# Attention passed SBUF to SBUF, w2's transpose moved, b2's gradient from ScalarE: one change to a transformer block's forward and backward pass

## The chip, the cores and the metric

The kernel runs on one core of a Trainium2 chip. A core has five engines that run side by side and meet at semaphores: TensorE (PE in the profile; PEld is its weight load), VectorE (DVE), ScalarE (ACT), GpSimd (POOL) and SyncE (SP). DMA transfers are issued from the queues of SP, POOL and ACT and are carried out by 16 DMA engines. The metric is the device time in microseconds of one execution; lower is better.

## The reference

One transformer block, forward and backward, in bfloat16, with S = 2048 positions, D = 512, F = 1792, and 32 heads of 16:

```python
h  = x + A(layernorm(x), wqkv, wo)
h2 = h + B(layernorm(h), w1, b1, w2, b2)

def A(x, wqkv, wo):            # W = 8 keys per query, 2 positions apart
    q, k, v = split(x @ wqkv)
    logits = einsum("bhsd,bhswd->bhsw", q, gathered k) * 16 ** -0.5
    logits = where(idx >= 0, logits, -1e9)      # idx = pos - 2 * (0..7)
    o = einsum("bhsw,bhswd->bhsd", softmax(logits), gathered v)
    return o @ wo

def B(x, w1, b1, w2, b2):
    return gelu(x @ w1 + b1) @ w2 + b2
```

The outputs are h2 and, for a given grad_out, the gradients of x, wqkv, wo, w1, b1, w2 and b2. The gradient of b2 is the sum of grad_out over the 2048 positions.

## The kernel before

The positions are worked on in four chunks of 512 (`CH`, `NC`). Most tiles have 128 partitions. The tile framework places waits and buffers, and orders each engine's instructions when the program is built; on the chip that order is fixed, so an instruction that waits holds up all behind it on its engine or queue. A tag with `bufs` buffers is a ring: a new tile waits until the readers of the old one are done.

Forward, per chunk c: `f_ln1` and `f_qkv` make q, k and v; `f_attn(c)` makes the softmax weights in two halves i (products `pa`, summed on PE into `lg`; `e`, exp on ACT, row sums `sm`, then `attn[c]`); `f_o(c)` multiplies the weights with v (`pbo`, eight products of 1.14 us pitch on DVE, L330), sums on PE (`pso`), copies to `otm` on ACT and transposes to `oT`; `f_h(c)` multiplies with wo, adds x, and makes the second layernorm and its transpose `ln2T`; `f_ffn1(c)` makes gelu in seven groups (ACT writes u, square and sigmoid; DVE z and g; POOL stores u, s and g to DRAM for the backward pass), and `f_ffn2(c)` multiplies with w2. The order in which they are written interleaves chunks: f_o(2), f_h(2), f_attn(3), then ffn1(2) mixed with ffn2(1), f_o(3), f_h(3), and so on.

The attention weights stand in `attn[c]` with 32 rows by four quarters in one layout, and the sums need them in `a4`, another spread over the partitions. Before, POOL stores them to DRAM (`at_r`, four DMAs, `put_q`, L442), and SP loads them back as `a4` (four DMAs, `att4`, L300); `a4` has one buffer. The backward pass reads at_r as well. `e` has two buffers of 2 KB a partition.

w2 is loaded twice: as it is (L587, on POOL, gated by exp of chunk 1) and transposed by a DMA on SP (L602, `w2T`, into the room of wqkv), held back by `gate(..., ("e", 3, 1))` until the second exp of chunk 3 has run. `turn_w_gen` transposes the four weights for the backward pass on PE, through one PSUM buffer (tag T), and stores them; it is taken in two steps of two.

Backward, first part (from about 282 us): `make_goutT` transposes grad_out on PE (through the same T buffer; ACT copies each pair of blocks, 128x1024, to SBUF, `to_T`, L276); `b1_gg` makes the gradient behind gelu, `b1_gx` that of the layernorm, and `gw2_gen`, taken step by step between, the gradient of w2. gw2_gen begins with b2's gradient: 16 matmuls of a column of ones with grad_out (L659), one copy on ACT and one store.

```python
    def f_o(c):
        a4 = att4(fr, at_r, CJ * c, CJ, f"a4_{c}", "a4", 1, 0)
```

Of the kernel before, what the change touches and what calls it, by code (L numbers as in the profile page):

```python
# [35 lines left out]
def kernel(  # L36
# [74 lines left out]
    def gate(ins, key):  # L111
        behind(ins, mark[key])
# [10 lines left out]
    nc.vector.memset(one_t[:], 1.0)  # L123
    ones_row = const.tile([1, P], BF16, name="ones_row")
    nc.vector.memset(ones_row[:], 1.0)
    ones_col = const.tile([P, 1], BF16, name="ones_col")
    nc.vector.memset(ones_col[:], 1.0)
    rstd1 = const.tile([P, NT], F32, name="rstd1")
    rstd2 = const.tile([P, NT], F32, name="rstd2")
    b1c = const.tile([P, FT], F32, name="b1c")  # L130
# [134 lines left out]
            nc.vector.tensor_scalar(out=dst[:, j, :], in0=src[:, j, :], scalar1=mv[:, j, 0:1],  # L265
                                    scalar2=r[:, j:j + 1], op0=ALU.subtract, op1=ALU.mult)

    def to_T(src, dst, nm, tag, tag2=None):
        for d2 in range(DC // 2):
            pt = ptile(f"pt{nm}{d2}", tag2 if tag2 and d2 else tag)  # L270
            for i in range(2):
                for j in range(TC):
                    dc = 2 * d2 + i
                    nc.tensor.transpose(pt[:, (i * TC + j) * P:(i * TC + j + 1) * P],
                                        src[:, j, dc * P:(dc + 1) * P], ident[:])
            nc.scalar.copy(out=dst[:, 2 * d2:2 * d2 + 2, :], in_=pt[:].rearrange("p (i t) -> p i t", i=2))  # L276


    def four(eng, pool_, d_t, t0, nj, name, tag, bufs, step, key=None):
# [63 lines left out]
    PRA, PRB = 4, 3  # L343
    oTs, hs, l2T = {}, {}, {}

    lT, k4s, q4s = {}, {}, {}

    def f_ln1(c):
        x = xs.pop(c)
# [67 lines left out]
    def f_attn(c):  # L417
        if c not in k4s:
            f_halo(c)
            f_k4(c)  # L420
            f_q4(c)
        k4, q4 = k4s.pop(c), q4s.pop(c)
        for i in range(TC // 2):
            lg = ltile(f"lg{c}_{i}")
            dots(fr, lg, q4, k4, i, f"{c}_{i}", HP[c], STEP[c])
            l4 = lg[:].rearrange("p j (w h) -> p j w h", w=W)
            mx = const.tile([P, 2, H], F32, name=f"mx{c}_{i}", tag="mx", bufs=2)
            nc.vector.tensor_reduce(out=mx[:], in_=lg[:].rearrange("p j (w h) -> p j h w", w=W), axis=AX.X, op=ALU.max)
# [11 lines left out]
            nc.vector.tensor_tensor(out=attn_v(c, i), in0=e[:],  # L440
                                    in1=sm[:].unsqueeze(2).to_broadcast([P, 2, W, H]), op=ALU.mult)
        put_q(pq, at_r, c, attn[c][:].rearrange("p s j m -> p s (j m)"))  # L442

    def f_o(c):
        a4 = att4(fr, at_r, CJ * c, CJ, f"a4_{c}", "a4", 1, 0)
        otm = fr.tile([P, TC, D], BF16, name=f"otm{c}", tag="qkv", bufs=2)
        for qd in range(Q4):
            v4 = row4(fr, v_r, qd, PAD + CJ * c - 2, CJ + 2, f"v4_{c}{qd}", "w4", 4, 0)
            ps = acc(f"pso{c}_{qd}")
            wsum(fr, ps, a4, v4, 0, f"o{c}_{qd}")  # L450
            mark["o", c, qd] = nc.scalar.copy(out=otm[:, :, qd * P:(qd + 1) * P], in_=ps[:].rearrange("p (j m) -> p j m", j=TC))
        pq.dma_start(out=tm(otm_d[c * CH:(c + 1) * CH, :]), in_=otm[:])
        oT = fr.tile([P, G, CH], BF16, name=f"oT{c}", tag="t2", bufs=2)
        to_T(otm, oT, f"o{c}", "U")
        oTs[c] = oT

    def f_h(c):
        x, oT = load_x(c, "xr"), oTs.pop(c)
        h = fb.tile([P, TC, D], BF16, name=f"h{c}", tag="h", bufs=2)
        for j in range(TC):  # L460
            ps = acc(f"psh{c}_{j}")
            for g in range(G):
                nc.tensor.matmul(ps[:], lhsT=oT[:, g, j * P:(j + 1) * P], rhs=wo[:, g, :], start=(g == 0), stop=(g == G - 1))
            nc.vector.tensor_tensor(out=h[:, j, :], in0=ps[:], in1=x[:, j, :], op=ALU.add)
        ln2 = fr.tile([P, TC, D], BF16, name=f"ln2_{c}", tag="t1", bufs=1)
# [125 lines left out]
    f_h(1)  # L591
    f_attn(2)
    turn_w = turn_w_gen()
    take(turn_w, 2)
    zero_pads(((q_r, S), (go_r, S), (at_r, S), (gl_r, S)), ("e", 1, 0))
    mix(f_ffn1(1), f_ffn2(0))
    f_o(2)
    f_h(2)
    take(turn_w, 2)
    f_attn(3)  # L600
    w2T = fw.tile([P, DC, F], BF16, name="w2T", tag="wq", bufs=1)
    gate(sync.dma_start_transpose(out=w2T[:], in_=B_w2[:, :]), ("e", 3, 1))  # L602
    mix(f_ffn1(2), f_ffn2(1))
    f_o(3)
    f_h(3)
# [10 lines left out]
    gb2 = br1.tile([1, D], BF16, name="gb2")  # L616
    for c in b1_order:
        gout[c] = br1.tile([P, TC, D], BF16, name=f"gout{c}")
    br2 = pool("br2", 1, side="right")

    def load_gout(c):
# [4 lines left out]
    def make_goutT(i):  # L626
        if i < NC:
            c = b1_order[i]
            goutT[c] = get(br1, [P, DC, CH], BF16, f"goutT{c}", "goutT", 2)
            to_T(gout[c], goutT[c], f"e{c}", "T")  # L630

    w1T_load = sync.dma_start_transpose(out=w1T[:], in_=B_w1[:, :])
    gate(w1T_load, ("r", 3))
# [20 lines left out]
        nc.vector.tensor_tensor(out=out_ap, in0=u[:], in1=resid, op=ALU.add)  # L654

    def gw2_gen():
        ps = acc("psb2", "A")
        for t in range(NT):
            nc.tensor.matmul(ps[0:1, :], lhsT=ones_col[:], rhs=gout[t // TC][:, t % TC, :], start=(t == 0), stop=(t == NT - 1))  # L659
        nc.scalar.copy(out=gb2[:], in_=ps[0:1, :])  # L660
        nc.scalar.dma_start(out=out_7.rearrange("(a d) -> a d", a=1), in_=gb2[:])
        for ft in range(FT):
            gtm = get(br1, [P, NT, P], BF16, f"gtm{ft}", "gtm", 2)
            sync.dma_start_transpose(out=gtm[:], in_=g_d[ft * P:(ft + 1) * P, :])
# [350 lines left out]
```

## Time and profile before

| what | us |
|---|---|
| five runs: 716.57, 715.1, 711.06, 714.37, 718.03; median | 715.1 |
| the profiled execution, its own time | 717.97 |
| its span, first to last instruction | 715.8 |
| PE busy (88% of the span) | 630.1 |
| DVE busy (78%) | 556.3 |
| ACT busy (55%) | 395.3 |
| POOL busy (29%) | 209.3 |

A row of a timeline reads: start, duration, engine, line, operation, output <- input, shapes, count, and in brackets how long the engine sat idle before and what ended that. A row of a tile's view reads: line, engine, operation, output <- input, count, then shortest, median and longest duration in ns, first and last start. PE's busy time counts overlapping matmuls once; one of 512 columns takes 379 ns from its start to its end, and a new one starts every 0.216 us. The granted clock is that of TensorE, 1.00 when full.

### The profile page before, as it was taken

How to read it: one execution, taken by the hardware profiler on the slowest of the kernel's cores; microseconds unless marked ns; L12 is line 12 of the kernel's file. 1: busy time of each engine (PE TensorE's matmuls, PEld its weight loads, DVE VectorE, ACT ScalarE, POOL GpSimd, SP SyncE). 2: the span in 40 equal slices, each digit the busy share in tenths (PEclk: the TensorE clock that was granted, in tenths of full speed). 3: DMA queues.
4: the chain of work that ended last, by engine and by line, in shares of the span. 5: the costliest groups of instructions: out<-in, count | busy, mean ns of one | idle time of the engine just before them, and what ended most of it. 6: DMA issues, size and time to landing. Idle time of an engine off the chain costs nothing.

```text
span 715.8 us, 10332 instructions
## 1 busy us (share of the span) xinstructions
PE 630.1 (88%) x3682; PEld 265.4 (37%) x3682; DVE 556.3 (78%) x919; ACT 395.3 (55%) x548; POOL 209.3 (29%) x318
## 2 busy tenths in 40 slices
PE   1898668779698499999999999999989999999985
PEld 0433222234243134444445444443523333334342
DVE  6467958778973849975988888386979999999655
ACT  4654325878957739945867676551222135357453
POOL 4324323534533432452443432313200310001000
PEclk9999897979989789999999999999999999999999
DMA  8497698664889769566775985849879998986632
GB/s 235 140 265 231 188 375 283 230 248 161 255 291 219 226 165 231 166 212 231 213 209 93 218 179 151 258 119 273 295 294 384 333 322 285 344 279 221 166 83 66
DMA packets 103221, 163.57 MB, mean 229 GB/s; under 512 B 60961, under 2 KB 69250, under 8 KB 103170
## 3 DMA queue, kind: packets, MB, share of 16 engines
q1 hardware_dynamic: 73824, 78.40, 39.2%
q0 software_dynamic: 24720, 80.07, 34.3%
q10 hardware_dynamic: 4626, 4.46, 1.9%
q8 instruction: 28, 0.46, 0.3%
q14 instruction: 23, 0.19, 0.1%
HBM read 90.97 MB, written 56.71 MB: 206 GB/s over the span
## 4 chain that ended last, share of the span: by engine, by line
PE 41%; DVE 18%; DMA 13%; issue 13%; ACT 9%; POOL 3%; SPq 2%; POOLq 0%; DVEq 0%; ACTq 0%
PE psy L892 5%; PE psw L788 5%; PE psq L370 4%; PE psq L929 4%; PE psw L667 3%; DVE pb L330 3%; PE psx L719 2%; DVE pa L313 2%; PE psf L506 2%; PE ps L535 2%; PE ga L320 2%; PE pss L336 2%; DMA v<-v_r 2%; DMA out_dram<-ow 2%; PE lg L320 1%
## 5 line engine op out<-in xcount | busy, mean ns | idle before, releaser
L330 DVE TENSOR_TENSOR pb<-ba,r 128x2048 bf16<-128x2048 bf16 x96 | 111.4, 1216 | 1.5 <-PE pss L336 1.0
L506 PE MATMUL psf<-ln2T,w 128*128 128x512 bf16 x224 | 58.9, 400 | 12.4 <-ACT u L508 12.3
L535 PE MATMUL ps<-w,g 128*128 128x512 bf16 x224 | 55.8, 379 | 0.0
L788 PE MATMUL psw<-h1tm,ln2a 128*128 128x512 bf16 (+1 forms) x256 | 54.3, 354 | 0.0
L667 PE MATMUL psw<-gout,gtm 128*128 128x512 bf16 x208 | 51.3, 379 | 1.8 <-DMA gtm<-g_d 1.0
L719 PE MATMUL psx<-w1T,gh 128*128 128x512 bf16 x216 | 50.4, 379 | 0.0
L330 DVE TENSOR_TENSOR pbo<-a,v 128x2048 bf16<-128x2048 bf16 x32 | 38.2, 1217 | 15.0 <-DMA a<-at_r 10.5
L372 ACT CAST qkv<-psq 128x512 bf16<-128x512 f32 x48 | 27.6, 586 | 32.7 <-PE psq L370 26.1
L697 PE MATMUL psg<-goutT,w2T 128*128 128x512 bf16 x168 | 42.3, 379 | 0.0
L508 ACT ACTIVATE u<-psf,b1c 128x512 bf16<-128x512 f32 x56 | 36.0, 681 | 8.5 <-PE psf L506 5.1
L313 DVE TENSOR_TENSOR pag<-go,bv 128x2048 bf16<-128x2048 bf16 x24 | 28.6, 1218 | 10.4 <-DMA go<-go_r 6.8
L506 PEld LDWEIGHTS <-w 128*128 128x128 bf16 x224 | 21.0, 101 | 42.1 <-issue 24.7
L710 POOL DMA_DIRECT2D h1tm_d<-th x27 | 20.6, 762 | 53.0 <-ACT th L708 37.2
L518 ACT ACTIVATE s<-z 128x1024 bf16<-128x1024 bf16 x28 | 29.6, 1060 | 11.7 <-DVE z L516 7.3
L863 ACT ACTIVATE gt<-pss 128x512 bf16<-128x512 f32 x32 | 19.1, 597 | 29.6 <-PE pss L336 29.6
L788 PEld LDWEIGHTS <-ln2a 128*128 128x128 bf16 x256 | 22.6, 98 | 29.8 <-issue 12.3
L708 ACT COPY th<-pth 128x1024 bf16<-128x1024 bf16 x27 | 27.0, 999 | 11.0 <-PE pth L706 11.0
L689 ACT ACTIVATE by<-bu 128x1024 bf16<-128x1024 bf16 x21 | 22.2, 1056 | 19.1 <-DVE gb1p L699 16.5
L892 PE MATMUL psy<-wqkvT,gT 128*128 128x512 bf16 x128 | 32.2, 383 | 0.1
L929 PE MATMUL psq<-gt,ln1a 128*128 128x512 bf16 x128 | 32.0, 380 | 0.0
L526 POOL DMA_DIRECT2D g_d<-g x28 | 20.6, 734 | 36.5 <-DVE g L520 34.5
L336 PE MATMUL pss<-pb,sel 128*32 128x512 bf16 x384 | 29.5, 384 | 1.5 <-DVE pb L330 1.2
(221 smaller groups left out, 1364.6 us busy)
## 6 DMA issues: line engine op xcount, KB each, us to landing
v<-v_r SPq DMA_DIRECT2D x16, 576.0 KB, 6.9
r<-go_r SPq DMA_DIRECT2D x16, 576.0 KB, 8.5
r<-k_r SPq DMA_DIRECT2D x16, 576.0 KB, 6.2
r<-q_r SPq DMA_DIRECT2D x16, 576.0 KB, 5.4
g_d<-g POOLq DMA_DIRECT2D x28, 256.0 KB, 4.0
h1tm_d<-th POOLq DMA_DIRECT2D x27, 256.0 KB, 4.4
h1tm<-h1tm_d POOLq DMA_DIRECT2D x3, 2048.0 KB, 13.6
x_d<-u POOLq DMA_DIRECT2D x21, 256.0 KB, 5.5
```

The costliest lines, as they stand in the source:

```text
L313: nc.vector.tensor_tensor(out=pr[:], in0=_ap(q_ap, [q_ap.ap[0], [P, 2], [0, W], [1, P]]), in1=_ap(k_ap, [k_ap.ap[0], [P, 2], [-DIL * P, W] ...
L330: last = nc.vector.tensor_tensor(out=pr[:], in0=_ap(a_ap, [a_ap.ap[0], [2 * H, CJ], [0, Q4], [1, H]], off=wh * H + (4 * H * wh if sg else 0)),
L336: mm = nc.tensor.matmul(ps[PR * n:PR * n + PR, :], lhsT=sel4[:], rhs=prs[wh][:, TC * n:TC * n + TC, :, :].rearrange("p j d h -> p (j d h)" ...
L506: nc.tensor.matmul(ps[:], lhsT=w1[0][:, dc, ft * P:(ft + 1) * P], rhs=ln2T[:, dc, :], start=(dc == 0), stop=(dc == DC - 1))
L508: nc.scalar.activation(out=u[:, i, :], in_=ps[:], func=ACT.Identity, bias=b1c[:, ft:ft + 1], scale=1.0)
L535: nc.tensor.matmul(ps[:], lhsT=gs[ft // 2][:, ft % 2, j * P:(j + 1) * P], rhs=w2[0][:, ft, :], start=(ft == 0), stop=False)
L667: nc.tensor.matmul(ps[:], lhsT=gtm[:, t, :], rhs=gout[t // TC][:, t % TC, :], start=(t == 0), stop=(t == NT - 1))
L697: nc.tensor.matmul(ps[:], lhsT=w2T[:, dc, ft * P:(ft + 1) * P], rhs=gT[:, dc, :], start=(dc == 0), stop=(dc == DC - 1))
L719: nc.tensor.matmul(ps[:], lhsT=t1s[ft // 2][:, ft % 2, j * P:(j + 1) * P], rhs=w1T[:, ft, :], start=(ft == 0), stop=(ft == FT - 1))
L788: nc.tensor.matmul(ps[:, 0:nf * P], lhsT=ln2a[:, t // TC, t % TC, dc * P:(dc + 1) * P], rhs=tmx[:, t, 0:nf * P], start=(t == 0), stop=(t = ...
L892: nc.tensor.matmul(ps[:], lhsT=gT[sel][:, g, j * P:(j + 1) * P], rhs=wqkvT[:, sel * G + g, :], start=(n == 0), stop=(n == NJ - 1))
L929: nc.tensor.matmul(ps[:], lhsT=ln1a[t // TC][:, t % TC, dc * P:(dc + 1) * P], rhs=gts[sel, t // TC][:, t % TC, :], start=(t == 0), stop=(t ...
```

## The change

Three parts. First, `f_attn` copies each half of the weights on DVE into a new tile `back`, with the four quarters in reverse order, and four DMAs on SP (`across`, which was there for q and k) carry `back` to `a4` from SBUF to SBUF. The stores to at_r stay, for the backward pass alone. `back` shares the two buffers of `e`; in the built program `back` has one of them and every `e` the other. Second, w2T is issued before `f_attn(3)`, gated by the h of chunk 1, and turn_w_gen is taken in steps of three and one. In the built program w2T stands on SP ahead of the transfers of a4 for chunk 2; POOL's load of w2 (L587), whose lines are not changed, comes ahead of the at_r stores of chunk 1. Third, ACT copies the transposed grad_out in halves that also give their row sums (`accum_out`), into `gb2p`; at the end of the stage the sums are added over the chunks, transposed on PE and stored. The matmuls with ones are gone.

```diff
-    def to_T(src, dst, nm, tag, tag2=None):
+    def to_T(src, dst, nm, tag, tag2=None, sums=None):
...
-            nc.scalar.copy(out=dst[:, 2 * d2:2 * d2 + 2, :], in_=pt[:].rearrange("p (i t) -> p i t", i=2))
+            if sums is None:
+                nc.scalar.copy(out=dst[:, 2 * d2:2 * d2 + 2, :], in_=pt[:].rearrange("p (i t) -> p i t", i=2))
+            else:
+                for i in range(2):
+                    nc.scalar.activation(out=dst[:, 2 * d2 + i, :], in_=pt[:, i * CH:(i + 1) * CH], func=ACT.Copy,
+                                         accum_out=sums[:, 2 * d2 + i, :])
...
             nc.vector.tensor_tensor(out=attn_v(c, i), in0=e[:],
                                     in1=sm[:].unsqueeze(2).to_broadcast([P, 2, W, H]), op=ALU.mult)
+            if i == 0:
+                back = fr.tile([P, Q4, TC, 2 * H], BF16, name=f"back{c}", tag="e", bufs=2)
+            o_ap, i_ap = back[:, 0, 2 * i, :], attn[c][:, 0, 2 * i, :]
+            st = 2 * H * TC
+            nc.vector.tensor_copy(out=_ap(o_ap, [o_ap.ap[0], [st, Q4], [1, 4 * H]]),
+                                  in_=_ap(i_ap, [i_ap.ap[0], [-st, Q4], [1, 4 * H]], off=(Q4 - 1) * st))
+        a4s[c] = fr.tile([P, CJ, 2 * H], BF16, name=f"a4_{c}", tag="a4", bufs=1)
+        across(a4s[c], back)
         put_q(pq, at_r, c, attn[c][:].rearrange("p s j m -> p s (j m)"))
 
     def f_o(c):
-        a4 = att4(fr, at_r, CJ * c, CJ, f"a4_{c}", "a4", 1, 0)
+        a4 = a4s.pop(c)
...
-            nc.vector.tensor_tensor(out=h[:, j, :], in0=ps[:], in1=x[:, j, :], op=ALU.add)
+            mark["h", c] = nc.vector.tensor_tensor(out=h[:, j, :], in0=ps[:], in1=x[:, j, :], op=ALU.add)
...
-    take(turn_w, 2)
+    take(turn_w, 3)
     zero_pads(((q_r, S), (go_r, S), (at_r, S), (gl_r, S)), ("e", 1, 0))
     mix(f_ffn1(1), f_ffn2(0))
     f_o(2)
     f_h(2)
-    take(turn_w, 2)
+    take(turn_w, 1)
+    w2T = fw.tile([P, DC, F], BF16, name="w2T", tag="wq", bufs=1)
+    gate(sync.dma_start_transpose(out=w2T[:], in_=B_w2[:, :]), ("h", 1))
     f_attn(3)
-    w2T = fw.tile([P, DC, F], BF16, name="w2T", tag="wq", bufs=1)
-    gate(sync.dma_start_transpose(out=w2T[:], in_=B_w2[:, :]), ("e", 3, 1))
...
-            to_T(gout[c], goutT[c], f"e{c}", "T")
+            to_T(gout[c], goutT[c], f"e{c}", "T", sums=gb2p[:, :, c:c + 1])
...
     def gw2_gen():
-        ps = acc("psb2", "A")
-        for t in range(NT):
-            nc.tensor.matmul(ps[0:1, :], lhsT=ones_col[:], rhs=gout[t // TC][:, t % TC, :], start=(t == 0), stop=(t == NT - 1))
-        nc.scalar.copy(out=gb2[:], in_=ps[0:1, :])
-        nc.scalar.dma_start(out=out_7.rearrange("(a d) -> a d", a=1), in_=gb2[:])
...
             br2.release()
             bt = pool("bt", 1)
+            nc.vector.tensor_reduce(out=gb2s[:], in_=gb2p[:], axis=AX.X, op=ALU.add)
+            nc.vector.tensor_copy(out=gb2b[:], in_=gb2s[:])
+            pth = ptile("ptg2", "T")
+            nc.tensor.transpose(pth[0:DC, 0:P], gb2b[:, :], ident[:])
+            nc.scalar.copy(out=gb2r[:], in_=pth[0:DC, 0:P])
+            pq.dma_start(out=out_7.rearrange("(dc p) -> dc p", p=P), in_=gb2r[:])
```

More of the change, by code (lines that the diff above doesn't have):

```diff
@@ L125 @@
     nc.vector.memset(ones_row[:], 1.0)
-    ones_col = const.tile([P, 1], BF16, name="ones_col")
-    nc.vector.memset(ones_col[:], 1.0)
     rstd1 = const.tile([P, NT], F32, name="rstd1")
@@ L344 @@
     oTs, hs, l2T = {}, {}, {}
-    lT, k4s, q4s = {}, {}, {}
+    lT, k4s, q4s, a4s = {}, {}, {}, {}
     def f_ln1(c):
@@ L615 @@
     place(br1, [P, D], BF16, "ow2", 3)
-    gb2 = br1.tile([1, D], BF16, name="gb2")
     for c in b1_order:
         gout[c] = br1.tile([P, TC, D], BF16, name=f"gout{c}")
+    gb2p = br1.tile([P, DC, NC], F32, name="gb2p")
+    gb2s = br1.tile([P, DC], F32, name="gb2s")
+    gb2b = br1.tile([P, DC], BF16, name="gb2b")
+    gb2r = br1.tile([DC, P], BF16, name="gb2r")
     br2 = pool("br2", 1, side="right")
```

## The prediction

> **What bounds the kernel now.** I read first the busy time by stretch (columns: length, busy us of PE, PEld, DVE, ACT, POOL, then granted clock, DMA share, GB/s), to see where TensorE (PE) is not full.
>
> ```profile
> 100.00:120.00 20.00, 12.16 (x61) 4.41 (x60) 12.80 (x20) 6.88 (x11) 4.32 (x7) 0.74 0.85 321
> 160.00:180.00 20.00, 19.98 (x107) 8.12 (x106) 17.48 (x30) 16.43 (x19) 8.21 (x12) 1.00 0.46 153
> 180.00:200.00 20.00, 13.42 (x109) 5.92 (x107) 19.05 (x27) 19.12 (x26) 11.51 (x16) 0.92 0.89 285
> 220.00:230.00 10.00, 10.00 (x46) 4.13 (x45) 2.41 (x4) 8.57 (x10) 3.63 (x5) 1.00 1.12 279
> 230.00:240.00 10.00, 3.68 (x11) 1.21 (x9) 7.87 (x11) 4.27 (x6) 3.13 (x5) 0.72 0.30 96
> 240.00:250.00 10.00, 5.22 (x46) 1.58 (x48) 8.88 (x12) 8.66 (x12) 5.55 (x8) 0.84 0.94 301
> 300.00:360.00 60.00, 59.25 (x346) 27.37 (x344) 46.14 (x106) 36.65 (x45) 25.68 (x37) 1.00 0.66 212
> 360.00:440.00 80.00, 78.11 (x454) 37.33 (x453) 68.65 (x160) 57.53 (x76) 31.34 (x45) 1.00 0.80 175
> ```
>
> From 300 on PE is full: work taken from PE there is time. In the forward it has holes, the largest at 230 to 250 (11.1 us idle). The timelines of SP, DVE and PE say what ends it:
>
> ```profile
> 94.92 4.49 SPq L300 DMA_DIRECT2D a<-at_r  x4
> 105.45 1.22 DVE L330 TENSOR_TENSOR pbo<-a,v 128x2048 bf16<-128x2048 bf16 x1 [4.03 <-DMA a<-at_r]
> ...
> 213.88 0.69 DVE L440 TENSOR_TENSOR attn<-e,sm 128x512 bf16<-128x512 f32 x1
> 210.94 9.82 SPq L602 DMA_TRANSPOSE w2T<-in_B_w_dram  x1
> 226.41 2.39 SPq L300 DMA_DIRECT2D a<-at_r  x4
> 231.33 1.22 DVE L330 TENSOR_TENSOR pbo<-a,v 128x2048 bf16<-128x2048 bf16 x1 [6.44 <-DMA a<-at_r]
> 236.95 3.57 PE L506 MATMUL psf<-ln2T,w 128*128 128x512 bf16 x8 [6.32 <-ACT u L508]
> ```
>
> Attention of chunk 3 is done at 214.5, its weighted sum (pbo) starts at 231.3: 16.8 us for SBUF to DRAM to SBUF, because w2T (issued 210.94, landing 16.7 later, at 227.6) fills the DMA engines (share 1.12). DVE's order is fixed, so z and g of ffn1(2) wait behind pbo, ACT's s behind them, PE behind u. Chunk 1 has the same in small (4.03). Chunks 0 and 2 show no such wait. The total:
>
> ```profile
> DVE pbo L330 <- DMA a<-at_r: 10.5, 2, 6.4
> ```
>
> **The change part by part**, in this profile's times; which instruction waits for which is read from the built program.
>
> *Chunk 1 (95 to 113).* The load of a_1 no longer waits for the at_r stores, but for the second copy into `back` (about 87) and for a4's only buffer, free when pbo of chunk 0 ends, 92.1. On SP it stands behind xr (86.87 to 88.8). Four issues at 0.6 (the row of k_first<-qkv, the same kind of transfer, 603 to 652 ns; landing 3.9 to 4.5) end at 94.5 and land by 99. DVE comes to pbo at 101.3: the 4.03 is gone. Late next is v_11, issued behind a_1 at 94.6 in place of 99.5; at the stretch's worst landing, 8.6, it is there at 103.2, just before its use. pbo stands ahead of chunk 0's layernorm, so all of ffn1(0) moves. On POOL the order also changes: the w2 load goes ahead of the at_r stores, as soon as the last reader of `early` is done (77.3 instead of 88.87). Two stores of at_r, four of q_r and two more of at_r queue behind it, but nobody in the forward waits for at_r now, and w2 no longer meets w1 (94.87). It meets the k_r stores at 82.5 instead, which xr waits behind; xr lands at 92.3 to 94 and is needed at 96.3, 2 us of cover. Bounds: 0 (w1 or v is late anyway) to 5.0 (4.03 and 1 more through v and q_r); nearer to the stall itself: **-3.5**.
>
> *Chunk 2 (156 to 214), w2T moved.* On SP w2T passes the loads of a_2, v_30..33, four output stores and xr. It waits for the last h of chunk 1 (157.1) and for 16 more PE transposes and two ACT copies (1.0 each) of the third weight, moved from 181 to 189 to where PE does ffn2(0). PE's order and the 1.7 us turn of the one T buffer put the last transpose at 162.8. So w2T issues 163 to 172.8 and lands at 179.7, while DMA share was 0.46: quieter, that holds. Against it: `e` has lost its second buffer to `back`, so e(2,1) waits for attn(2,0) and its copy. attn(2,1) moves from 167.5 to 171.4, its copy ends at 172.8, and a_2 issues 172.8 to 175.2 behind w2T. How long it then takes, bounds: 4.3 (a_3 in before, at the tail of w2T) to 9.9 (at_r stores beside w2T). Beside w2T it is nearer to the second: about 181.7. pbo(2) started at 179.4, so 2.3 late; behind it wait g_0, g_1 and with them u's ring. DVE still owes 1.0 more at that point (g_0, o, one reduction 2.15; pa 1.14 already done), and copies 0.35: 3.6 late at the end of pbo(2). Given back: ACT has two copies less (2.0) in a stretch where it is 19.1 of 20 busy, and PE's 13 score matmuls of chunk 3 (1.9) are no longer between the last pbo and psh. **+1.5**, between -1 (a_2 lands in 4.3) and +4 (nothing is given back).
>
> The Trainium skill speaks against this step too: "DMA: Bandwidth & Descriptors", section "Queues, rings and completion order", says that on each DMA engine descriptors are consumed in ring order, and SP has one ring there. By that rule a_2 can't overtake w2T: not before 179.7, and by the rule plus the 4.3 row 182 to 184, which would make this term about +2.
>
> *Chunk 3 (214 to 254).* attn(3,1) comes as before, right behind ln2(2), its copy (0.35) after it; a_3 issues over 2.4 and lands within 4.5: pbo at about 219 instead of 231.3 (both with chunk 2's delay left out). I then laid out DVE's and ACT's new order by row durations: pbo 1.14, z 0.34 and 0.60, g 0.60; u 1.2 a pair, square and sigmoid 0.96, table load 1.28, otm 0.5, oT 0.96. ACT then is the longer: 7 groups of 3.1, 4 otm, 2 oT, one load are 26.9 from u at 216.3, which with short waits ends oT at about 244 instead of 253.9. Late next: ACT itself. PE has 11.1 idle to give in 230 to 250. Bounds: -12 (DVE alone, 22 us of work from 219) to -4.5 (only the 6.44 stall, less two pbo of 1.14 that now stand ahead of z_0): **-9.5**, as ACT's rows are complete.
>
> *b2's gradient (282 to 345).*
>
> ```profile
> L659 PE MATMUL psb<-gout,ones_col x16: 377/378/379, 338.1 to 345.4; 128*1 128x512 bf16 x16
> 367.50 3.45 PE psw L667 x16
> L276 ACT COPY goutT<-pte x6: 988/1003/1012, 297.3 to 380.3; 128x1024 bf16<-128x1024 bf16 x6
> L646 ACT ACTIVATE luf<-psx x16: 576/597/604, 325.5 to 467.8; 128x512 f32<-128x512 f32 x16
> L646 ACT ACTIVATION_READ_ACCUMULATOR luf<-psx x16: 191/194/211, 326.0 to 468.3; 128x1 f32 x16
> ```
>
> Matmuls overlap; 16 of 512 columns cost 3.45 on the full PE (second line, from the chain): -3.45. Eight copies of 1.0 become 16 of 0.6 with 16 reads of 0.19: 4.6 us more on ACT, hidden where it is 61 to 72% busy (300 to 440), not in 289 to 300. There ACT's new order puts the second half of the first tile behind s, square and 1-s (3 x 0.96), and PE's transposes of the next tile wait for the one T buffer: pth(0) comes about 2 later. The other chunks: 0.4. The two small DVE ops, one transpose, copy and store at the end are beside gw2 (gb1's same ops took 0.2 each): 0. Bounds: -3.45 (all hidden) to +2. **-1.0**.
>
> *Copies into `back`*, 8 in all: no row of this shape; between 0.2 (the 14x128 copy, L834) and 0.62 (the strided 128x512 copy, L231). Taken 0.35, the pitch of a plain 128x512 bf16 op (L265, 4 in 1.38). Chunk 0's lie under DVE's 3.0 wait at 70.5; those of 2 and 3 are counted; chunk 1's: **+0.5**.
>
> Sum: -3.5 + 1.5 - 9.5 - 1.0 + 0.5 = -12.0. The profiled run took 717.97 (span 715.8), 2.9 over the median of 715.1: 706.0 for that run, **703** for the median.
>
> **Rivals.** (a) *Only stalls go*: ffn1's own chain holds chunk 3 and w1 holds chunk 1; -4.5 + 1.5 - 1 + 0.5 = -3.5, or -6 with 2.5 kept in chunk 1: 709 to 712. For: ACT 8.57 of 10 busy in 220 to 230. Against: it idles from 229.7 to 235.3. (b) *The ACT reads cost more than the matmuls*, +4 to +5 at 289 to 300: about 708. For: ACT is full there. Against: it is one turn of one buffer. (c) *Slower*: a_2 sits behind w2T so long that f_o(2) loses what f_o(3) gains. Its price is the landing of a_2 beyond 181.7, one for one, as DVE and ACT are full until 199; at the sum's -12 it decides from a landing 12 later, about 193.7, 19 us after issue, and shows as slower from 197. For: all DVE waits there. Against: the longest landing near, a q_r store, is 14.3. Price at 200: +6, 721. (d) *w2T doesn't move*, as it still waits for late transposes: excluded by the program's order, which has them before ln2(1). (e) *All shifts in full*, -12 and -5: 696.
>
> **How the numbers follow.** 0.5% (3.6 us) is what this kernel's runs can tell. Chances: forecast 0.56, a 0.19, b 0.12, c 0.06, e 0.07. Faster by over 0.5% (under 711.5): nearly all of the forecast, b and e, and half of a: 0.84; same 0.10; slower 0.06. Range: up to most of a (711), down to past e (695); c lies outside.
>
> **What would show it.** Right: no DVE wait for a at pbo of chunks 1 and 3; w2T issued near 160 (earlier by chunk 1's gain), PE busy over 7 of 10 in the stretch after ln2(2); PE's 16 psb gone, pth(0) late by 2. Wrong: a DVE wait of over 8 before pbo(2), or oT of chunk 3 following ln2T(2) by over 35 us (39.3 now, from 214.6 to 253.9), or psf waiting for w1 in chunk 0.

## The result, and the profile after

The changed kernel is slower, not faster: 720.8 us against 714.4 (medians of 28 and 47 executions), ratio 1.0078, 95% interval 1.0060 to 1.0095, that is 4.3 to 6.8 us more. All ratios here leave out slow executions, those over 1.5% above the fastest of their kernel (four of 28 of the changed kernel and none of the kernel before; four of twelve in run 15), so this one is below 720.8 over 714.4, which is 1.0090. Forecast were 703 and a gain of 12.

The traced execution of the changed kernel took 727.86, 7 over its own median, so of its numbers I use those that other traces repeat; run 4 below has the same forward code and a trace of 714.92, and stands beside it.

The first fence is SP's, ACT's, POOL's and DVE's timeline of the changed kernel, around chunks 1, 2 and 3 (start, duration, engine, line, operation, count, idle time before and what ended it; L598 is w2's load, L387 the transfer of back to a4):

```profile
80.28 1.12 POOL L598 DMA_DIRECT2D w<-in_B_w_dram  x1 [2.30 <-DMA v<-v_r]
81.95 2.18 SPq L177 DMA_DIRECT2D k_r<-qkv  x4
92.42 0.58 ACT L462 CAST otm<-pso 128x512 bf16<-128x512 f32 x1 [4.91 <-DMA k_r<-qkv]
97.79 3.21 SPq L387 DMA_DIRECT2D a<-back  x4
108.00 1.19 DVE L333 TENSOR_TENSOR pbo<-a,v 128x2048 bf16<-128x2048 bf16 x1
165.57 9.80 SPq L612 DMA_TRANSPOSE w2T<-in_B_w_dram  x1
176.16 4.45 SPq L387 DMA_DIRECT2D a<-back  x4
189.87 1.23 DVE L333 TENSOR_TENSOR pbo<-a,v 128x2048 bf16<-128x2048 bf16 x1 [9.62 <-DMA a<-back]
226.22 0.68 DVE L443 TENSOR_TENSOR attn<-e,sm 128x512 bf16<-128x512 f32 x1
232.68 2.36 DVE L333 TENSOR_TENSOR pbo<-a,v 128x2048 bf16<-128x2048 bf16 x2 [3.95 <-DMA a<-back]
```

Chunk 3 went nearly as forecast: pbo starts 6.5 after the start of the second half of attention, not 17.5, but a wait of 3.95 for a is left, where I had written down none. Chunk 1 has no wait for a any more, and yet its pbo starts at 108.00, where it was 105.45: now otm of chunk 0, the step before, is 6 us later, for it waits 4.91 for the k_r stores (3.91 in run 4). And chunk 2 has a new wait of 9.62 for a, which stands behind w2T (4.39 in run 4).

PE's holes lie elsewhere now. Busy time by stretch, first of the changed kernel and then of the kernel before (columns: length, busy PE, PEld, DVE, ACT, POOL, then granted clock, DMA share, GB/s):

```profile
180.00:200.00 20.00, 11.96 (x65) 4.47 (x64) 10.38 (x15) 11.22 (x13) 4.73 (x7) 0.82 0.77 197
200.00:220.00 20.00, 15.65 (x82) 6.71 (x83) 15.59 (x26) 17.36 (x23) 10.13 (x15) 0.76 0.93 329
230.00:240.00 10.00, 10.00 (x47) 4.25 (x45) 7.28 (x10) 9.63 (x12) 3.20 (x5) 1.00 0.38 118
240.00:250.00 10.00, 9.10 (x52) 3.40 (x50) 7.39 (x13) 9.68 (x14) 6.77 (x10) 1.00 0.93 294
```

```profile
200.00:220.00 20.00, 19.91 (x110) 8.62 (x103) 13.47 (x27) 10.69 (x13) 6.55 (x10) 0.91 0.90 258
```

230 to 250, where PE idled 11.1, is full (19.1 of 20). 200 to 220, which was full, has 4.4 idle, and 180 to 200, which had 6.6 idle before, has 8.0; DVE and ACT, which were full there, have 9 to 10 idle each. In run 4 the idle time of PE in the three is 4.6, 5.5 and 4.5.

Read from the ends of the transposes (ACT's rows), the pass divides into stretches. Each line is one traced execution; the ratio is over many.

| kernel | to ln2T(1) | ln2T(1) to ln2T(2) | ln2T(2) to oT(3) | the last two | ln2T(3) ends at | to first pth | ratio to the kernel before |
|---|---|---|---|---|---|---|---|
| before | 167.2 | 48.3 | 38.3 | 86.6 | 266.2 | 34.1 | 1 |
| changed | 171.9 | 57.7 | 29.7 | 87.3 | 271.8 | 37.0 | 1.0078 |
| run 4: changed, b2 by matmuls | 171.7 | 52.8 | 29.7 | 82.4 | 266.7 | 34.9 | 1.0022 |
| run 10: only attention | 170.0 | 51.0 | 30.2 | 81.2 | 263.2 | 34.2 | 1.0032 |
| run 11: only w2T | 167.9 | 56.2 | 29.7 | 85.9 | 265.8 | 34.4 | 1.0005 |
| run 9: only b2 | 166.9 | 47.9 | 37.9 | 85.8 | 265.0 | 37.0 | 1.0045 |
| run 3: changed, w2 later | 166.5 | 51.5 | 29.7 | 81.2 | 259.6 | 37.0 | 0.9972 |
| run 5: runs 2, 3 and 4 together | 167.8 | 48.5 | 34.7 | 83.2 | 263.5 | 34.2 | 0.9972 |
| run 6: runs 3 and 4 together | 166.9 | 51.2 | 29.7 | 80.8 | 260.3 | 35.0 | 0.9932 |
| run 15: only attention, w2 later | 163.1 | 47.5 | 36.8 | 84.3 | 259.7 | 34.1 | 1.0003 |
| run 7: before, w2 later | 166.5 | 52.6 | 31.8 | 84.4 | 263.2 | 34.2 | 0.9924 |
| run 8: before, one e | 169.9 | 51.2 | 30.1 | 81.3 | 263.1 | 34.4 | 0.9947 |

One trace is one draw: executions of one kernel differ by 1.5 to 4 us (standard deviation), and the changed kernel and run 4, with the same forward code, end ln2T(3) 5.1 apart. Verdicts below go by the ratios; the traces say where.

### The profile page after: what moved, and what is told of

Read it like the earlier page. It is cut to its first block, busy times and chain, and to the rows that moved or that the text cites. A ratio compares the mean times of both kernels' runs of the same rounds, so it can differ in the third digit from the quotient of the medians.

```text
span 726.1 us, 10328 instructions
## 1 busy us (share of the span) xinstructions
PE 634.6 (87%) x3667; PEld 266.5 (37%) x3667; DVE 556.6 (77%) x928; ACT 396.9 (55%) x572; POOL 210.0 (29%) x319
## 5 line engine op out<-in xcount | busy, mean ns | idle before, releaser
L517 PE MATMUL psf<-ln2T,w 128*128 128x512 bf16 x224 | 61.3, 412 | 10.1 <-ACT u L519 10.0
L676 PE MATMUL psw<-gout,gtm 128*128 128x512 bf16 x208 | 52.8, 388 | 7.3 <-DMA gtm<-g_d 5.5
L333 DVE TENSOR_TENSOR pbo<-a,v 128x2048 bf16<-128x2048 bf16 x32 | 38.2, 1214 | 22.7 <-DMA a<-back 13.6
L706 PE MATMUL psg<-goutT,w2T 128*128 128x512 bf16 x168 | 44.5, 393 | 0.0
L878 ACT ACTIVATE gt<-pss 128x512 bf16<-128x512 f32 x32 | 19.1, 596 | 27.3 <-PE pss L339 25.4
L708 DVE CUSTOM_DVE_ANT_0 gh<-psg,by 128x512 bf16<-128x512 f32 x42 | 27.9, 686 | 7.5 <-PE psg L706 7.0
L797 PEld LDWEIGHTS <-ln2a 128*128 128x128 bf16 x256 | 22.6, 98 | 28.4 <-issue 11.1
L676 PEld LDWEIGHTS <-gtm 128*128 128x128 bf16 x208 | 19.6, 99 | 34.7 <-issue 7.6
```

Source lines behind the costliest of these rows:

```text
L333: last = nc.vector.tensor_tensor(out=pr[:], in0=_ap(a_ap, [a_ap.ap[0], [2 * H, CJ], [0, Q4], [1, H]], off=wh * H + (4 * H * wh if sg else 0)),
L517: nc.tensor.matmul(ps[:], lhsT=w1[0][:, dc, ft * P:(ft + 1) * P], rhs=ln2T[:, dc, :], start=(dc == 0), stop=(dc == DC - 1))
L676: nc.tensor.matmul(ps[:], lhsT=gtm[:, t, :], rhs=gout[t // TC][:, t % TC, :], start=(t == 0), stop=(t == NT - 1))
L706: nc.tensor.matmul(ps[:], lhsT=w2T[:, dc, ft * P:(ft + 1) * P], rhs=gT[:, dc, :], start=(dc == 0), stop=(dc == DC - 1))
L797: nc.tensor.matmul(ps[:, 0:nf * P], lhsT=ln2a[:, t // TC, t % TC, dc * P:(dc + 1) * P], rhs=tmx[:, t, 0:nf * P], start=(t == 0), stop=(t = ...
```

## The experiments

**The three parts, one at a time.** Each of these kernels is the one before with one part of the change.

Run 9, b2's gradient alone:

```diff
-            to_T(gout[c], goutT[c], f"e{c}", "T")
+            to_T(gout[c], goutT[c], f"e{c}", "T", sums=gb2p[:, :, c:c + 1])
...
-        for t in range(NT):
-            nc.tensor.matmul(ps[0:1, :], lhsT=ones_col[:], rhs=gout[t // TC][:, t % TC, :], start=(t == 0), stop=(t == NT - 1))
...
+            nc.vector.tensor_reduce(out=gb2s[:], in_=gb2p[:], axis=AX.X, op=ALU.add)
...
```

> The kernel before with only b2's gradient taken from ScalarE's sums. Theory G (the 16 matmuls stood in a wait for the transposed g, gtm, and so cost nothing; the sums cost real time): PE waits 3 to 4 for gtm between 340 and 370, the first pth comes 36 to 38 after the last ln2T instead of 34.1, and the time is 3 to 5 over the kernel before: 718 to 720. Rival (my forecast): -1.0, 713 to 715. Rival order: the 4 between the two kernels with attention changed came from the order that the scheduler found there, and here it is 715 within 2.

Measured: 720.1 against 715.7, ratio 1.0045 (1.0004 to 1.0085), +3.2. The first pth comes 37.0 after the last ln2T, against 34.1. PE waits for gtm, the transposed g that the gradient of w2 needs, but 2.0 and not 3 to 4.

Run 10, attention alone:

```diff
+        a4s[c] = fr.tile([P, CJ, 2 * H], BF16, name=f"a4_{c}", tag="a4", bufs=1)
+        across(a4s[c], back)
...
-        a4 = att4(fr, at_r, CJ * c, CJ, f"a4_{c}", "a4", 1, 0)
+        a4 = a4s.pop(c)
```

> The kernel before with only attention's way changed; w2T's load and b2's gradient as before. What the other runs leave for it: the changed kernel less b2's part was 1.0022 of the kernel before, and putting w2T back changed nothing (1.0079 against 1.0078): 714 to 718. In the trace the wait of otm of chunk 0 for the k_r stores (4 to 5) with w2 issued near 80, and from ln2T(2) to oT(3) 30 instead of 38.3. Rival: w2T's new place cost 3 or more and the place of this kernel's own w2T none: 708 to 712.

Measured: 716.4 against 715.7, ratio 1.0032 (0.9996 to 1.0067), +2.3. Chunk 3's stretch is 8.1 shorter (30.2), chunk 2's 2.6 longer, and otm of chunk 0 waits 3.34 for the k_r stores; w2 is issued at 80.19.

Run 11, w2T's move alone:

```diff
-    take(turn_w, 2)
+    take(turn_w, 3)
...
-    take(turn_w, 2)
+    take(turn_w, 1)
+    w2T = fw.tile([P, DC, F], BF16, name="w2T", tag="wq", bufs=1)
+    gate(sync.dma_start_transpose(out=w2T[:], in_=B_w2[:, :]), ("h", 1))
     f_attn(3)
-    w2T = fw.tile([P, DC, F], BF16, name="w2T", tag="wq", bufs=1)
-    gate(sync.dma_start_transpose(out=w2T[:], in_=B_w2[:, :]), ("e", 3, 1))
```

> The kernel before with only w2T's load moved; a goes through DRAM and follows w2T on SP's queue in chunk 2. Theory: in chunk 3 the round trip no longer meets w2T, so pbo comes 8 to 11 after the second attn instead of 17.5, and that is worth up to 6.4; in chunk 2 a comes 2 to 5 later. Net -4 to 0: 711 to 715. Rival c of the prediction in its pure form (a behind w2T on one queue is late by 10): 718 or more, with a wait of over 8 ahead of pbo of chunk 2.

Measured: 715.5 against 715.7, ratio 1.0005 (0.9969 to 1.0041). Its timeline of SP and DVE in chunk 2:

```profile
163.13 13.54 SPq L601 DMA_TRANSPOSE w2T<-in_B_w_dram  x1
180.14 2.41 SPq L300 DMA_DIRECT2D a<-at_r  x4
187.66 1.23 DVE L330 TENSOR_TENSOR pbo<-a,v 128x2048 bf16<-128x2048 bf16 x1 [7.04 <-DMA a<-at_r]
```

w2T now keeps SP's queue busy from 163.1 to 176.7, a is issued behind it, and pbo starts 20.1 after the second half of attention (11.9 before). Chunk 2 takes 7.8 more and chunk 3 8.6 less: the stall has changed places, at no gain and no loss.

The three ratios add up to 1.0082; the change as a whole has 1.0078. So these runs show no fourth cost that only the three together make: +2.3, +0.4 and +3.2 of about 5.6. But each has an uncertainty of 2.5 to 2.9, so the sum has one of 4 to 5, and a cost or gain of that size could hide in it.

**The changed kernel with one thing undone.**

Run 1: w2T back at its old place in the code, with its old gate (run 11's diff the other way round).

> The changed kernel with w2T's load (and the fourth weight's transposes) put back where they were, behind attention of chunk 3 with its old gate; on SP's queue w2T then stands right ahead of chunk 3's a, not of chunk 2's. Theory Q (a stands behind w2T on SP's queue, and that alone makes it late): pbo of chunk 2 waits less than 2 us for a instead of 9.6 and starts near 181 to 184 (189.9 in the changed kernel); in chunk 3 the wait is back, pbo at 10 to 17 after the second attn, as in the kernel before (17.5). Sum against the kernel before: chunk 1 +2.3, chunk 2 0 to +2, chunk 3 -2 to 0: 714 to 719 us. Rival E (e's one buffer and the copies make attention of chunk 2 late, whatever w2T does): pbo of chunk 2 stays later than 187, oT of chunk 2 stays over 8 late, and with chunk 3's gain lost the time is 725 or more.

Measured: 721.1, ratio 1.0079 (1.0047 to 1.0110): the same as with w2T moved. The wait before pbo of chunk 2 is 0.45, as the first theory said, but chunk 3 stays short (30.0) although a now stands behind w2T there, and the time does not fall. Theory Q, that a's place behind w2T alone makes the loss, falls. Rival E falls too: pbo of chunk 2 is at 179.9, not after 187.

Run 2: w2T behind chunk 3's a.

```diff
-    take(turn_w, 1)
-    w2T = fw.tile([P, DC, F], BF16, name="w2T", tag="wq", bufs=1)
-    gate(sync.dma_start_transpose(out=w2T[:], in_=B_w2[:, :]), ("h", 1))
+    take(turn_w, 2)
     f_attn(3)
+    w2T = fw.tile([P, DC, F], BF16, name="w2T", tag="wq", bufs=1)
+    gate(sync.dma_start_transpose(out=w2T[:], in_=B_w2[:, :]), ("back", 3))
```

Here `mark["back", c]` is the copy into back, and turn_w is taken 2 and 2.

> As the one before, but w2T's load is gated behind the last copy into back of chunk 3, so that on SP's queue it follows a_3 and stands ahead of nothing that attention waits for. Theory Q: no wait of over 2 us for a in chunks 2 and 3; pbo of chunk 3 starts 5 to 7 us after its second attn instead of 17.5; chunk 3 gains 8 to 9, chunk 1 still costs 2.3, chunk 2 0 to 2: 706 to 711 us, about 0.8% under the kernel before. Rival C (contention: w2T's transfer fills all the DMA engines, and whatever is in flight beside it is late, in front of it in the queue or behind): pbo of chunk 3 waits over 4 us for a or v, or psg of the backward waits for w2T, and the time is 714 or more.

Measured: 718.4 against 715.1, ratio 1.0035 (1.0009 to 1.0061). Nothing that attention needs stands behind w2T now, and that is worth 0.43% of the changed kernel (0.3 to either side), not the 706 to 711 of theory Q.

Run 3: the gate of w2's load.

```diff
-    gate(pq.dma_start(out=w2[0][:], in_=B_w2.rearrange("(ft p) d -> p ft d", p=P)), ("e", 1, 0))
+    gate(pq.dma_start(out=w2[0][:], in_=B_w2.rearrange("(ft p) d -> p ft d", p=P)), ("o", 0, 0))
```

> The changed kernel with one key altered: the load of w2 waits for the first otm of chunk 0 instead of the first e of chunk 1, and so no longer stands ahead of attn's stores on POOL's queue. Theory: in the changed kernel w2's 1.8 MB (issued 80.3) meet the k_r stores (82.0), which land in 7.5 instead of 4.1 (medians); otm of chunk 0 waits 4.9 for them, as it takes over their buffer. Without that, otm(0) starts at 87 instead of 92.4, pbo of chunk 1 at 101 to 104 instead of 108.0, and the time falls by 3 to 6 from the changed kernel's 720.8: 715 to 718. Rival: the two big loads w1 and w2 meet again, psf of chunk 0 or ps of its second half waits for its weight, and the time stays at 720 or more.

Measured: 714.9, ratio 0.9972 (0.9941 to 1.0003), 1.06% or 7.6 us less than with the old gate. otm of chunk 0 is at 88.75 and no longer waits for the stores, which land in 2.6 (median of chunk 1's four, as far as the profile tells their landings; 8.9 in the changed kernel, 2.2 before, and not the 7.5 and 4.1 that I had written). pbo of chunk 1 starts at 105.2 (108.0 in the changed kernel; I had expected 101 to 104), and oT of chunk 1 is 4.2 earlier.

Run 4: b2 by matmuls again, the rest of the change kept (run 9's diff the other way round).

> The changed kernel with b2's gradient taken by the 16 matmuls again and the copies of goutT whole again. My step: the new way is worth 1.0, so this one is 1 slower: 721 to 723. Rival b of the prediction: ScalarE's 16 halves and 16 reads cost more than the matmuls (first pth 3.0 later, counted from the last ln2T: 35.1 before, 38.1 in the changed kernel), and this one is 1 to 3 faster: 718 to 720, with the first pth 35 after the last ln2T.

Measured: 716.8, ratio 1.0022 (0.9993 to 1.0052), 0.56% or 4.0 less than the changed kernel. The first pth is back at 34.9 after ln2T(3). Rival b of the prediction, at about its price there, and more than the 1 to 3 expected here.

**Together, and on the kernel before.**

Run 5: the changed kernel with runs 2, 3 and 4 together. Run 6: with runs 3 and 4, w2T where the change puts it. Their common part:

```diff
-    gate(pq.dma_start(out=w2[0][:], in_=B_w2.rearrange("(ft p) d -> p ft d", p=P)), ("e", 1, 0))
+    gate(pq.dma_start(out=w2[0][:], in_=B_w2.rearrange("(ft p) d -> p ft d", p=P)), ("o", 0, 0))
...
-            to_T(gout[c], goutT[c], f"e{c}", "T", sums=gb2p[:, :, c:c + 1])
+            to_T(gout[c], goutT[c], f"e{c}", "T")
```

> Attention SBUF to SBUF kept, and the three losses taken out: w2's load waits for the first otm of chunk 0, w2T's load follows a_3 on SP's queue, b2's gradient goes by the 16 matmuls again. If the three add up as measured singly (7.6, 2.4 to 3 and 4.0 under the changed kernel's 720.8): 705 to 708, 1.0 to 1.3% under the kernel before. Rival: the gate's gain and w2T's place are the same microseconds seen twice (both give chunk 2 a quieter stretch), and it is 709 to 712.

> The same, but w2T's load stays where the change put it, ahead of chunk 2's a. If a's place behind w2T costs about 2 in chunk 2 (ln2T of chunk 1 to ln2T of chunk 2: 50.4 and 50.8 with w2T elsewhere, 51.5 and 52.8 with it there, in the four runs so far), this one is 1 to 3 over its neighbour: 708 to 711. If place on the queue is free, the two are the same; if a lands 10 late as in the changed kernel's profiled run (9.6 of wait), it is 714 or more.

Measured: 712.8, ratio 0.9972 (0.9938 to 1.0005), and 710.4, ratio 0.9932 (0.9907 to 0.9958). Run 3 and run 4 together promise 0.992 for run 6, and that holds. But run 5, with a free of w2T, should have been the faster one and is not: the two differ by 0.40%, with 0.42 to either side. By this pair, a's place on the queue is worth nothing that these runs can tell; run 15 below is another.

Run 7: the kernel before with w2's gate altered alone, run 3's diff.

> The kernel before, with only w2's gate altered (first otm of chunk 0 instead of first e of chunk 1). Theory: the gate only undoes a harm of the change (w2's load pulled from 88.9 to 80.3, into the k_r stores), so on the kernel before, where w2 is issued after those stores anyway, it gives nothing: 713 to 717. Rival: a later w2, behind w1, is a gain by itself, whatever attention does: 707 to 711, and then most of the 7.6 that the gate gave on the changed kernel says nothing of the change.

Measured: 710.7 against 715.3, ratio 0.9924 (0.9892 to 0.9955). My theory was that the gate only undoes a harm of the change; the rival holds. A later w2 is a gain of 5.4 by itself, and most of run 3's 7.6 says nothing of the change. Its timeline of POOL and DVE:

```profile
96.20 0.78 POOL L584 DMA_DIRECT2D w<-in_B_w_dram  x1 [0.28 <-issue]
97.71 1.10 POOL L587 DMA_DIRECT2D w<-in_B_w_dram  x1
103.78 1.23 DVE L330 TENSOR_TENSOR pbo<-a,v 128x2048 bf16<-128x2048 bf16 x1 [2.15 <-DMA a<-at_r]
```

w1 (L584) goes ahead of w2 (L587), and a of chunk 1 comes 1.7 earlier than before, through DRAM. With attention SBUF to SBUF and the same gate pbo of chunk 1 starts at 105.2, 106.9, 106.1 and 103.6 (runs 3, 5, 6 and 15): not earlier than that, but for run 15.

Run 8: one buffer for e in the kernel before.

```diff
-    place(fr, [P, 2, W, H], F32, "e", 2)
+    place(fr, [P, 2, W, H], F32, "e", 1)
...
-            e = get(fr, [P, 2, W, H], F32, f"e{c}_{i}", "e", 2)
+            e = get(fr, [P, 2, W, H], F32, f"e{c}_{i}", "e", 1)
```

> The kernel before with one buffer for e instead of two, as the change leaves it (the other holds back). Theory: the two halves of attention of chunk 2 then come 7 to 9 apart (5.7 before; 7.2 to 8.9 in the changed kernel and its variants), and chunk 2 from ln2T(1) to ln2T(2) takes 49 to 51 instead of 48.3; nothing else: 716 to 718. Rival: with the round trip through DRAM still there, the second half's delay goes straight into a: 720 or more. Or there is slack, and it is 715 like the kernel before; then the 2 that chunk 2 loses with w2T at its old place come from the copies and across itself.

Measured: 711.9 against 715.3, ratio 0.9947 (0.9918 to 0.9977): faster, where the theories had it slower or the same. The halves of attention of chunk 2 come 8.7 apart (5.7 before) and chunk 2 takes 51.2, as foreseen; but chunk 3 takes 30.1 in place of 38.3, with the trip through DRAM in place.

Run 12: the diffs of runs 7 and 8 together.

> The kernel before with w2's gate altered and one buffer for e, each of which was faster by itself (0.9924 and 0.9947). If they take away different waits (the gate: w2 ahead of w1 and beside chunk 1's a; the one buffer: chunk 3's part, 30.1 instead of 38.3 from ln2T(2) to oT(3)), they add: 705 to 708. If both only shake the order that the scheduler found, so that the wait of 6.4 in chunk 3 falls elsewhere, it is gained once: 710 to 712.

Measured: 710.1 against 715.7, ratio 0.9916 (0.9878 to 0.9953). They do not add up; what the two gain is largely one and the same. It is the lowest ratio of all, but its interval overlaps those of runs 6 and 7.

**What was still open.** Run 13 takes the matmuls of b2 away and puts only a copy of one row of grad_out in their place, so that its gradient of b2 is not one:

```diff
-        ps = acc("psb2", "A")
-        for t in range(NT):
-            nc.tensor.matmul(ps[0:1, :], lhsT=ones_col[:], rhs=gout[t // TC][:, t % TC, :], start=(t == 0), stop=(t == NT - 1))
-        nc.scalar.copy(out=gb2[:], in_=ps[0:1, :])
+        nc.scalar.copy(out=gb2[:], in_=gout[3][0:1, 0, :])
```

Run 14 is run 9 with those lines kept, up to the copy to `gb2`, which is not stored:

```diff
     def gw2_gen():
+        ps = acc("psb2", "A")
+        for t in range(NT):
+            nc.tensor.matmul(ps[0:1, :], lhsT=ones_col[:], rhs=gout[t // TC][:, t % TC, :], start=(t == 0), stop=(t == NT - 1))
+        nc.scalar.copy(out=gb2[:], in_=ps[0:1, :])
```

> The kernel before without the 16 matmuls of b2's gradient and with nothing in their place (out_7 gets a row of grad_out): what taking them away is worth by itself. Theory G (they stand in a wait for gtm): 0 to -1.5 against the kernel before, 714 to 716, and the trace shows PE waiting 2 or more for gtm between 340 and 365, where the kernel before waits less. My step: -3.45, 711 to 712.

> The kernel before with the sums of the change and with the 16 matmuls kept as well (their result goes nowhere): what the sums cost by themselves. Theory G: about as much as the change of b2's part alone (1.0045), +2 to +4, 717 to 719, the first pth 36 to 38 after the last ln2T. My step: +0.4 to +2, 715.5 to 717. Rival: the cost lies in the order without the matmuls (psw and its gtm earlier), and with them in place it is 715 within 1.

Measured: run 13 713.4 against 714.3, ratio 0.9984 (0.9954 to 1.0014), -1.1; run 14 717.7, ratio 1.0056 (1.0031 to 1.0081), +4.0. So the sums cost 4.0 by themselves. Run 13's -1.1 is not the worth of the matmuls, for the copy in their place has a cost of its own. ACT and PE in run 13:

```profile
275.68 0.62 ACT L657 COPY gb<-gout 1x512 bf16<-1x512 bf16 x1 [5.81 <-DMA gout<-in_grad_out_dram]
278.82 3.34 PE L506 MATMUL psf<-ln2T,w 128*128 128x512 bf16 x8 [3.91 <-ACT u L508]
```

The copy stands on ACT in the middle of ffn1(3) and waits there for grad_out, u comes late behind it, and PE waits for u; in the kernel before the copy that closes b2's gradient runs at 345.9, without a wait. The first pth comes 38.2 after ln2T(3), 4.1 later than before. And the wait for gtm between 340 and 365, which the theory had, is not there. What the matmuls are worth is left to run 9 against run 14, which differ by them alone: 1.0045 against 1.0056, 0.8 us less without them, with 3.4 to either side.

Run 15: attention alone with w2's gate altered, the diffs of runs 10 and 3 on the kernel before.

> The kernel before with attention SBUF to SBUF and w2's gate on the first otm of chunk 0, w2T and b2 as before: against the kernel before with the gate alone (0.9924) it tells what attention's new way is worth once w2's load is out of its way. If 0, as the pair with w2T moved says (0.9932): 0.990 to 0.996, 709 to 712. If the 8 that chunk 3 gains come through and only w2 had eaten them: 0.985 or less, under 705. If the copies and e's one buffer cost something: 0.997 or more.

Measured: 717.3 against 714.3, ratio 1.0003 (0.9963 to 1.0044). Beside run 7 (0.9924), attention's new way does not gain once w2 is out of its way: it costs 0.8%, with 0.5 to either side. But w2T is in its way here. SP and DVE in chunk 3, whose second half of attention starts at 208.9:

```profile
205.73 10.74 SPq L615 DMA_TRANSPOSE w2T<-in_B_w_dram  x1
216.58 2.54 SPq L389 DMA_DIRECT2D a<-back  x4
224.72 1.23 DVE L335 TENSOR_TENSOR pbo<-a,v 128x2048 bf16<-128x2048 bf16 x1 [6.89 <-DMA a<-back]
```

pbo starts 15.8 after that, with no trip through DRAM: nearly the old stall. Run 6 is this kernel with w2T moved, and has 0.9932: here the move is worth 0.7%, with 0.5 to either side, where the pairs of runs 4 and 10, of run 1 and the changed kernel, and of run 11 and the kernel before show 0.1% or less.

## Why the prediction was wrong, point by point

**Chunk 1, forecast -3.5 (0 to -5.0): wrong in sign.** The step that failed is "It meets the k_r stores at 82.5 instead, which xr waits behind; xr lands at 92.3 to 94 and is needed at 96.3, 2 us of cover." I asked who waits behind the stores on the queue, and not who waits for the room that the stores read. otm of chunk 0 has the tag of the qkv tiles (two buffers) and can't be written before k_r has been read out. It had waited for that 0.21 before, so the cover was nothing:

```profile
86.26 0.58 ACT L451 CAST otm<-pso 128x512 bf16<-128x512 f32 x1 [0.21 <-DMA k_r<-qkv]
```

That row was in the profile. In the changed kernel the wait is 4.91 (3.91 and 3.34 in runs 4 and 10), pbo of chunk 0 ends at 97.8 in place of 92.1, and a_1, which needs a4's only buffer, is issued at 97.79 instead of the 92 that the step had. Up to ln2T(1) that is +2.8 to +5.1 in the traces of changed attention with w2 early (runs 1, 2, 4, 10 and the changed kernel), and -4.2 to +0.6 with it late (runs 3, 5, 6, 15). Not all of it need be this wait: run 8, with one e and none of the rest, has +2.6 there. And the gain that was to be had wasn't the way's: with w2 late, a comes 1.7 earlier through DRAM too (run 7). Without the wait another size of the step fails, "land by 99": in runs 3, 5, 6 and 15 the last of a's four transfers is issued between 95.1 and 96.9 and lands 8.3 to 10.2 later, beside w1 and w2, which are issued between 94.5 and 97.3; I had taken 3.9 to 4.5 from a row of another stretch, while a itself, at 94.92 in the kernel before, had taken 6.5 to 6.9 (and 8.6 was not the stretch's worst landing: w1 took 14.7).

**Chunk 2, forecast +1.5 (-1 to +4): too small.** +4.4 in run 4's trace and +9.3 in the changed kernel's. The order on the queue held: in the trace of run 4 w2T is issued at 165.58 and lands 16.9 later, at 182.5, and pbo starts at 184.4 on a's arrival. So did it in every trace with a behind w2T: a was there 1.5 to 5.3 after w2T's landing (runs 1, 3, 4, 6, 10, 11, 15 and the changed kernel). The Trainium skill's rule on this ("DMA: Bandwidth & Descriptors", section "Queues, rings and completion order"), that each DMA engine takes descriptors in ring order and SP has one ring there, agrees with that order. The same section adds that a later descriptor may finish its write before an earlier one, so "can't overtake" was more than it says. Nor was it a better guide to the size: my 181.7 was 2.0 after the landing that I forecast for w2T, and by the rule it was 2.3 to 4.3, both within what was measured. What I missed is that w2T is issued later than the 163 that I had, 2.6 in run 4, and that w2T's own time is no constant, 11.1 to 19.9 from issue to landing over these traces, and that chunk 2 grows by 2.6 with no w2T in it (run 10).

**Chunk 3, forecast -9.5 (-4.5 to -12): right in size, -8.6 in the changed kernel and run 4.** But it was not a gain to be added to chunk 2's loss. The 38.3 of the kernel before shrink to 30 to 32 in every trace here in which chunk 2 takes 50 or more, whatever was changed: by w2T's move alone (29.7), by one buffer for e (30.1), by w2's gate (31.8). Where chunk 2 stays at 47.5 or 48.5 (runs 15 and 5, both with attention changed), chunk 3 keeps 36.8 and 34.7. The failing step is the sum itself, "-3.5 + 1.5 - 9.5": chunks 2 and 3 are to be read as one stretch. There the forecast was -8; measured are -4.2 (run 4), -5.4 (run 10), -0.8 (run 11) and +0.7 (the changed kernel's trace). Kernels with one forward code differ there by 5 (run 4 and the changed kernel) or by 1 (86.6 before, 85.8 in run 9), so the smaller of these are not told from nothing. I had read the stall of 16.8 as time that was the trip's and w2T's. The part of the trip is small where w2T is ahead: in runs 1, 10 and 15, from SBUF to SBUF, pbo starts 2.5 to 2.9 after w2T's landing at 221.2 to 222.2, whether the second half of attention starts at 208.9 or at 214.7. And run 8 shows that with the trip in place, and w2T ahead of it, the same two stretches can be 81.3, though its pbo still starts 13.1 after the second half.

Rival c, which I gave 0.06, named the right place, a behind w2T, and the sign that I wrote down for it, a wait of over 8 before pbo(2), came up (9.62). But it isn't what made the kernel slower: with w2T back (run 1) the time is the same.

**b2's gradient, forecast -1.0 (-3.45 to +2): wrong in sign, +3.2 by itself and +4.0 within the change.** One term is "-3.45", the matmuls' time, and the step behind it "From 300 on PE is full: work taken from PE there is time." Without the sums it may have held: from the first pth to the last matmul run 13's trace takes 402.6, where the ten traces with the matmuls and without the sums take 404.3 to 411.3. But in all five traces with the sums and without the matmuls (the changed kernel and runs 1, 2, 3 and 9) PE waits for gtm between 356 and 368, by 2.0 to 4.8; in run 14, with both, and in all traces without the sums there is no such wait. So of the 3.45 most or all comes back as a wait for the next input of gw2, a term that I had put at nothing. In run 9:

```profile
359.81 0.60 PE L668 MATMUL psw<-gout,gtm 128*128 128x512 bf16 x2 [2.01 <-DMA gtm<-g_d]
```

That is read from traces; by the ratios the matmuls are worth 0.8 with 3.4 to either side (runs 9 and 14), which shows neither 0 nor 3.45.

The other term is "pth(0) comes about 2 later. The other chunks: 0.4", +2.4 in all, measured +4.0 (run 14, 2.2 to 5.8). pth was 3.0 later in every trace with the sums, as in run 14's rows of ACT: four halves with their reads of the sums stand between the last 1-s (296.94) and the first pth, and the second tile's halves wait for the one T buffer.

```profile
297.98 0.58 ACT L280 ACTIVATE goutT<-pte 128x512 bf16<-128x512 bf16 x1
298.45 0.20 ACT L280 ACTIVATION_READ_ACCUMULATOR goutT<-pte 128x1 f32 x1
300.11 0.60 ACT L280 ACTIVATE goutT<-pte 128x512 bf16<-128x512 bf16 x1 [0.88 <-PE pte L274]
300.61 0.19 ACT L280 ACTIVATION_READ_ACCUMULATOR goutT<-pte 128x1 f32 x1
302.07 1.01 ACT L716 COPY th_first<-pth 128x1024 bf16<-128x1024 bf16 x1 [0.69 <-PE pth L714]
```

From the first pth to the last matmul that trace takes 408.5, the kernel before 408.2, so in this pair the 3.0 reach the end in full; but as this stretch varies by 7 from trace to trace, the price rests on run 14's ratio. This is rival b, with the place, the mechanism and nearly the price (+4 to +5) that I had written down, and a chance of 0.12. The argument against it, "one turn of one buffer", was true of the place of the delay and beside the point, for little slack lay behind it.

**The copies into back, +0.5:** 0.28 to 0.35 each in the changed kernel, as estimated. One buffer for e, which I had charged 4 us in chunk 2, costs nothing on balance (run 8).

**The total.** Of attention and w2T together I forecast -11; run 4 shows +1.6 (-0.5 to +3.7). Of that, chunk 1 lost what it was to gain, and chunks 2 and 3 gave 4.2 to 5.8 instead of 8 in the traces of runs 3, 4 and 6, and nothing in the changed kernel's. Two small sums of the prediction do not come out as written, and neither decides anything: 6.44 less two pbo of 1.14 is 4.2 and not 4.5, and -12 and -5 with the other terms kept give 699 for rival e and not 696. What is not settled: by run 10's trace the forward pass ends 3.0 earlier than before, and by run 15's 6.5, and neither kernel is faster in its ratio; in run 15 the backward part of that trace takes 3.2 more than before, in run 10 3.1 less (its traced execution was 5 under its median), so whether the backward part gives the time back or these were lucky traces the runs don't say. Nor is it shown why a later w2 or one e makes the kernel before faster; only that the built programs then have another order on DVE, ACT and POOL, and where in the trace the time is less.

## What to carry to other kernels

When a load moves, list the transfers that it will run beside, and for each of them who reuses the memory that they read or write, not only who is behind them on a queue; a row whose wait is 0.2 has no cover. A stall that ends one chunk's stretch is not a gain until the neighbouring stretches are added to it: build the kernel with that part alone, and the one with an unrelated small change of order as a control, before pricing it. Work taken from a full engine is time only if what follows on that engine is ready, so look first whether its next input comes from a DMA. And a stand-in for what is taken out has waits of its own: look up its row before the run is used as a price.

## What the runs showed of the hardware that I had not expected

A hole in PE can be paid for twice. In the changed kernel PE waited for gtm in the backward part, and the granted clock was 0.82 to 0.83 for 20 us after a stretch of 1.00 (in run 3, after a wait of 3.60 there, 0.83 for 10 us); run 4, without that wait, kept 1.00. Not every hole does it: after a wait of 2.01 there run 9 kept 1.00. Columns as above; the changed kernel, then run 4:

```profile
367.72 1.03 PE L676 MATMUL psw<-gout,gtm 128*128 128x512 bf16 x2 [3.32 <-DMA gtm<-g_d]
```

```profile
360.00:370.00 10.00, 6.68 (x28) 2.67 (x27) 5.40 (x12) 4.20 (x5) 4.18 (x6) 0.83 1.11 209
370.00:380.00 10.00, 10.00 (x51) 4.81 (x49) 6.60 (x14) 5.05 (x5) 3.38 (x5) 0.82 1.03 183
```

```profile
360.00:370.00 10.00, 9.87 (x58) 4.70 (x57) 8.63 (x21) 6.90 (x10) 4.97 (x7) 1.00 1.12 218
370.00:380.00 10.00, 10.00 (x54) 4.76 (x53) 8.63 (x19) 5.81 (x12) 3.46 (x5) 1.00 1.12 282
```

The transposing load w2T, of one size in all kernels, kept SP's queue busy for 6.9 to 13.5 us and landed 11.1 to 19.9 after its issue; what sets the difference is not shown. And changes of one gate or one buffer, which remove no work, moved the time by 0.5 to 0.8%, as much as the whole change under study.
